# Tokens on 128 partitions with the last 64 apart, and batch 1's queries in 512-byte pieces turned by TensorE, in a fused packed-attention and expert kernel on one core

## The chip, the core and the metric

The kernel runs on one core of a Trainium2 chip. The metric is the device time of one execution in microseconds (us). Before the change it is 443.84 us, the median of three runs (443.28 to 444.25). Engines are named as in the profile: PE is TensorE, PEld its weight load, DVE is VectorE, ACT is ScalarE, POOL is GpSimd, SP is SyncE (here it issues nearly every DMA).

## What is computed

There are 8 batches, 8 heads, 576 tokens, head width 64. All is float32.

```python
def _attn_ref(q, k, v, p):                 # q, k, v: (8, 8, 576, 64); p: (8, 8, 32, 64)
    p_packed = sm_attn(p, k, v)            # 32 pack queries look at 576 keys
    out = sm_attn(q, p_packed, p_packed)   # 576 queries look at the 32 packed rows
def _moe_ref(x, w_gate, w_local, w1, w2):  # x: (8, 576, 512), the heads side by side
    logits = x @ w_gate                    # 8 experts
    # a token takes its own best expert, or its predecessor's, by a local gate; the first its own
    h = np.maximum(x[b, s] @ w1[e], 0.0)   # w1: (8, 512, 1024)
    out[b, s] = p[e] * (h @ w2[e])         # w2: (8, 1024, 512)
```

## The kernel before

The expert of a batch's first token is read back by the program (`choose`, L641: the number `e` is written by DVE and loaded into a register of SP), and only then can SP ask for that expert's weights. All 576 tokens of the batch are run through this one expert; a branch after the main program redoes what strays from it.

For each batch the work has two sides. The *main* side is the expert: `layer1` (L917) and `layer2` (L945 to L954) over 16 steps, eight chunks of 128 hidden rows for each of two token halves (320 and 256 tokens); `relu` (L928 on ACT, L932 on DVE) stands between them, and `splits` (L903 on ACT, L905 on DVE) makes a high and a low part of each chunk of `w2`. The *side work* prepares a later batch: load (`loads`), turn the keys so that the head width lies on partitions (`turn_keys`, L395 on DVE; for batch 1 `turn_tokens`, L376 on PE and L381 on ACT), `scores` (L428 matmul, L436 and L447 on DVE), `keys` (exponential L464, transposes L474, copies L479, the product with the values L493, normalising L505, transpose L513, copy L514 to `ppT`), turn the queries (`turn_queries`, L527 on DVE; for batch 0 `turn_tokens`), `queries` (L543, L563), the softmax over 32 packed rows (`soften`, L581 to L607, nearly all on DVE), `gates` (L699 to L783, which holds the choice `e`), and `pack_weights` (L877, L888, L891), which multiplies the packed values into `w1`. Batch 0 has its own path: keys turned by DVE (L362), an early choice from token 0 alone (`early_choice`, L654 to L687), `w1` in four quarters (`pack_quarters`, L848 to L860), queries in two parts.

The order of the instructions is not written out. A planner (`Clock`, `weave`) walks generators; each `need(...)` says which tiles, buffers (`slot`) and PSUM banks a step waits for, and the planner gives out the step whose modelled time has come: loads first, then side work, oldest batch first, then the main side. Its prices are a few constants: DMA bytes over `clock.rate` (GB/s), a line for each engine. Each engine then runs what it was given in that order. `BUFS` has the buffers of each tag: `kv` holds keys, values and first queries, `qn` the turned or to-be-turned keys and queries. While the main side has not begun, matmuls on a constant (L216, `keep_warm`) fill PE's gaps.

SP's order of batch 0's weights is the list `FIRST`: `1` a quarter of `w1`, `2` a chunk of `w2`, `v` batch 1's values, `q` half of batch 1's queries. `load_tokens` brings keys or values as 96 partitions of six tokens (1,536-byte pieces), `load_pairs` batch 0's queries as 96 partitions with two tokens side by side (512-byte pieces), `load_blocks` all later queries and keys in 128-byte pieces, already in the blocks that DVE's transpose wants. Three conditions matter here: `turn_keys` waits for `sts[0]["quads"][0] == NQ` (long true after batch 0), `turn_queries` for the tiles `a2t` of its batch, which come free when the batch before has issued its gate matmuls (L699, `give(*a2t)`), and `scores` takes two PSUM banks for each of two head groups `Q`, both at once for batch 1 (four banks).

## Time and profile before

| | us |
|---|---|
| median of 3 runs | 443.84 |
| the profiled execution | 441.43 |
| its span, first to last instruction | 439.7 |
| PE busy (matmuls on the constant among it) | 417.1 (21.5) |
| DVE, ACT, POOL busy | 303.5, 177.1, 27.1 |
| mean granted TensorE clock | 0.984 of full |

A view by windows gives, for each stretch, the busy time of each engine with its number of instructions, then the granted TensorE clock (1.00 is 2.4 GHz, 0.50 is 1.2 GHz), the share of the 16 DMA engines that was busy, and the rate. A line of the timeline has the start, the length, engine, line, operation, tiles, how many were merged, and in brackets how long the engine had sat idle and what ended that. DMA issues appear under the queue that issues them (SPq).

### The profile page before, as it was taken

How to read it: one execution, taken by the hardware profiler on the slowest of the kernel's cores; microseconds unless marked ns; L12 is line 12 of the kernel's file. 1: busy time of each engine (PE TensorE's matmuls, PEld its weight loads, DVE VectorE, ACT ScalarE, POOL GpSimd, SP SyncE). 2: the span in 40 equal slices, each digit the busy share in tenths (PEclk: the TensorE clock that was granted, in tenths of full speed). 3: DMA queues.
4: the chain of work that ended last, by engine and by line, in shares of the span. 5: the costliest groups of instructions: out<-in, count | busy, mean ns of one | idle time of the engine just before them, and what ended most of it. 6: DMA issues, size and time to landing. Idle time of an engine off the chain costs nothing.

```text
span 439.7 us, 10378 instructions
## 1 busy us (share of the span) xinstructions
PE 417.1 (95%) x4030; PEld 335.3 (76%) x4031; DVE 303.5 (69%) x862; ACT 177.1 (40%) x409; POOL 27.1 (6%) x44
## 2 busy tenths in 40 slices
PE   9998999768999989999999899998999999999995
PEld 8886788455887768877887578786887788878884
DVE  4586779848886488777967597747887688537231
ACT  1554533236434352435543353235342553335121
POOL 0000010300020000200020003000011001100000
PEclk9999999958999999999999999999999999999999
DMA  8989999472999479982899669991999640454011
GB/s 187 224 263 234 160 176 133 89 288 97 204 125 249 156 225 151 165 288 82 197 131 163 259 179 167 135 346 61 223 132 159 258 142 6 162 185 145 0 60 54
DMA packets 165078, 73.17 MB, mean 166 GB/s; under 512 B 133024, under 2 KB 145056, under 8 KB 165024
## 3 DMA queue, kind: packets, MB, share of 16 engines
q1 hardware_dynamic: 162752, 72.04, 77.1%
q8 instruction: 33, 0.54, 0.6%
q10 hardware_dynamic: 2272, 0.41, 0.6%
q14 instruction: 21, 0.17, 0.2%
HBM read 63.00 MB, written 9.44 MB: 165 GB/s over the span
## 4 chain that ended last, share of the span: by engine, by line
PE 77%; DVE 9%; DMA 9%; issue 2%; ACT 1%; SPq 1%; POOLq 0%; DVEq 0%; POOL 0%; ACTq 0%
PE bank L945 35%; PE bank L917 20%; DMA w1t<-in_moe_w_dram 4%; PE bank L950 3%; PE bank L954 3%; DMA qn<-in_q_dram 3%; PE bank L216 3%; PE bank L474 2%; PE bank L493 2%; PE bank L543 2%; DVE qn L527 2%; PE bank L428 2%; DVE wpl L891 2%; DMA kv<-in_q_dram 2%; PE bank L877 1%
## 5 line engine op out<-in xcount | busy, mean ns | idle before, releaser
L945 PE MATMUL bank<-w2s,h 128*128 128x512 f32 x768 | 204.0, 398 | 4.2 <-DVE w2s L905 2.5
L945 PEld LDWEIGHTS bank<-w2s,h 128*128 128x128 f32 x768 | 136.1, 188 | 32.7 <-issue 4.0
L932 DVE SCALAR_TENSOR_TENSOR h<-bank,h 128x256 fp32r<-128x256 f32 x192 | 61.5, 348 | 67.5 <-ACT h L928 67.4
L928 ACT ACTIVATE h<-bank 128x256 fp32r<-128x256 f32 (+1 forms) x128 | 52.9, 413 | 133.8 <-PE bank L917 127.5
L917 PEld LDWEIGHTS bank<-a2h,wph 128*128 128x128 f32 x256 | 47.0, 188 | 16.8 <-issue 1.9
L917 PE MATMUL bank<-a2h,wpl 128*128 128x320 f32 (+1 forms) x256 | 56.6, 299 | 2.3 <-DVE wpl L891 2.3
L917 PE MATMUL bank<-a2h,wph 128*128 128x320 f32 (+1 forms) x256 | 56.7, 302 | 0.0
L917 PE MATMUL bank<-a2l,wph 128*128 128x320 f32 (+1 forms) x256 | 54.8, 295 | 0.0
L917 PEld LDWEIGHTS bank<-a2h,wpl 128*128 128x128 f32 x256 | 41.4, 188 | 4.2 <-DVE wpl L891 4.1
L607 POOL TENSOR_TENSOR a2l<-a2t,a2h 128x576 fp32r<-128x576 f32 (+2 forms) x17 | 23.1, 1360 | 330.5 <-ACT a2h L604 255.2
L905 DVE TENSOR_TENSOR w2s<-w2raw,w2s 128x512 fp32r<-128x512 f32 x64 | 41.8, 683 | 0.5 <-ACT w2s L903 0.5
L917 PEld LDWEIGHTS bank<-a2l,wph 128*128 128x128 f32 x256 | 41.0, 188 | 0.0
L903 ACT CAST w2s<-w2raw 128x512 fp32r<-128x512 f32 x64 | 37.6, 623 | 2.6 <-DMA w2raw<-in_moe_w_dram 2.5
L950 PE MATMUL bank<-w2s,h 128*128 128x512 f32 x64 | 25.6, 401 | 0.0
L954 PE MATMUL bank<-w2s,h 128*64 128x512 f32 x64 | 25.0, 390 | 0.0
L216 PE MATMUL bank<-warm 128*128 128x128 f32 x136 | 21.5, 305 | 1.1 <-DVE warm L211 1.1
L216 PEld LDWEIGHTS bank<-warm 128*128 128x128 f32 x136 | 18.9, 214 | 2.4 <-issue 1.6
L464 ACT ACTIVATE a<-a,nb 128x576 f32<-128x576 f32 x16 | 12.4, 777 | 20.5 <-DVE nb L447 20.5
L888 ACT CAST wph<-bank 128x512 fp32r<-128x512 f32 x28 | 15.1, 597 | 11.7 <-PE bank L877 11.5
L563 DVE STREAM_TRANSPOSE sT<-bank 128x288 f32<-128x288 f32 (+2 forms) x36 | 13.0, 417 | 9.0 <-ACT gate L561 9.0
L527 DVE STREAM_TRANSPOSE qn<-qn 128x1152 f32<-128x1152 f32 x14 | 19.1, 1369 | 0.0
L479 ACT COPY a1T<-bank 96x384 f32<-96x384 f32 x30 | 13.1, 477 | 14.4 <-PE bank L474 14.4
(126 smaller groups left out, 431.9 us busy)
## 6 DMA issues: line engine op xcount, KB each, us to landing
w2raw<-in_moe_w_dram SPq DMA_DIRECT2D x64, 256.0 KB, 6.0
w1t<-in_moe_w_dram SPq DMA_DIRECT2D x14, 1024.0 KB, 6.6
kv<-in_v_dram SPq DMA_DIRECT2D x16, 576.0 KB, 8.1
qn<-in_q_dram SPq DMA_DIRECT2D x28, 288.0 KB, 7.1
out_dram<-o SPq DMA_DIRECT2D x31, 256.0 KB, 2.4
qn<-in_k_dram SPq DMA_DIRECT2D x24, 288.0 KB, 8.1
kv<-in_k_dram SPq DMA_DIRECT2D x4, 576.0 KB, 5.7
w1t<-in_moe_w_dram SPq DMA_DIRECT2D x4, 512.0 KB, 7.4
```

The costliest lines, as they stand in the source:

```text
L216: nc.tensor.matmul(out=warm_ps[:, :128], lhsT=warm, rhs=warm, start=True, stop=True)
L527: nc.vector.transpose(out=qT, in_=qT)
L607: eng.tensor_tensor(out=a2l, in0=a2t, in1=a2h.bitcast(F32), op=ALU.subtract)
L888: nc.scalar.copy(out=hi[fh][:, Q], in_=ts[fh, Q])
L903: nc.scalar.copy(out=w[:, 0], in_=raw)
L905: nc.vector.tensor_tensor(out=w[:, 1], in0=raw, in1=w[:, 0].bitcast(F32), op=ALU.subtract)
L917: nc.tensor.matmul(out=t[:, :GROUP * (m1 - m0)], lhsT=st["wp"][c // 4][wi][:, Q, fs], rhs=a2[ai][Q][:, GROUP * m0:GROUP * m1], start=(n == ...
L928: nc.scalar.activation(out=h[:, :w], in_=t[:, :w], func=AF.Relu)
L932: nc.vector.scalar_tensor_tensor(out=h[:, dst:dst + z - a], in0=t[:, a:z], scalar=0.0, in1=h[:, a:z].bitcast(F32), op0=ALU.max, op1=ALU.su ...
L945: nc.tensor.matmul(out=acc, lhsT=hs[hi], rhs=w[:, wi], start=(c == 0 and n == 0), stop=(c == NC - 1 and n == 2),)
L950: nc.tensor.matmul(out=acc, lhsT=h[:, 256:WIDE + TAIL], rhs=w[:, 0], start=(c == 0), stop=False, skip_group_check=True,)
L954: nc.tensor.matmul(out=acc[0:TAIL], lhsT=h[:, 256:WIDE], rhs=w[:, 1], start=False, stop=(c == NC - 1), skip_group_check=True,)
```

## The change

Keys, values and batch 0's queries are loaded as 128 partitions of four tokens for the first 512 tokens (1,024-byte pieces; queries and batch 1's keys in two DMAs of 512-byte pieces), and the last 64 tokens apart (`rest`): one DMA more for each load, into tiles under the tag `o`, or for values into constant tiles `v_rest` whose upper half GpSimd clears once at the start. The score row is cut into four chunks of 128 and one of 64 instead of six of 96: five transposes for a head group instead of six, the copies redrawn (for batches from 1 on one of 128x512 and one of 64x128 instead of two of 96x384), and five chunks instead of six in the product with the values. Batch 0's scores go over four row groups instead of three, with extra matmuls for the last 64 tokens.

Batch 1's queries are no longer brought in 128-byte pieces inside `FIRST`; they are loaded after its keys by `load_pairs` and turned by PE and ACT (`turn_tokens`), and need not wait for `a2t`. `FIRST` has the values earlier, before the third and fourth quarter of `w1`. `kv` has five buffers. Batch 1's scores are given out for each head group by itself (two banks). From batch 2 on the turning of keys and queries waits until the choice of the batch before has been given out. Batch 0's `w2` chunks from the third on have their low part made by GpSimd. A copy of 8 logits in `early_choice` is gone. Batch 0's packs come in four copies, and three small loads move from ACT's queue to SP's, behind the values.

```diff
@@ BUFS, FIRST
-    "kv": 4, "qn": 3, ...
+    "kv": 5, "qn": 3, ...
-FIRST = "1 2 1 2 2 1 2 v 1 2 q 2 q 2 2".split()
+FIRST = "1 2 1 2 2 v 1 2 1 2 2 2 2".split()
...
@@ load_tokens (load_pairs alike, in two DMAs of 512-byte pieces and a rest)
-        x = tile_([TP, HQ, NJ * D], F32, "kv")
-        clock.rate = 255.0
-        nc.sync.dma_start(
-            out=x, in_=at(src, b).rearrange("(h q) (p c) d -> q p h (c d)", q=NQ, c=NJ)[Q],
-        )
-        return x
+        x = tile_([128, HQ, NJ * D], F32, "kv")
+        rest = tile_([TAIL, HQ, D], F32, "kt", "o") if rest is None else rest
+        rows = at(src, b).rearrange("(h q) s d -> q h s d", q=NQ)[Q]
+        clock.rate = 340.0
+        nc.sync.dma_start(out=x, in_=rows[:, 0:512].rearrange("h (p c) d -> p h (c d)", c=NJ))
+        clock.rate = 200.0
+        nc.sync.dma_start(out=rest[0:TAIL], in_=rows[:, 512:S].rearrange("h p d -> p h d"))
+        return x, rest
...
@@ loads
-            order = (("p", 1), ("k", 0), ("k", 1)) if st["second"] else \
+            order = (("p", 1), ("k", 0), ("k", 1), ("q", 0), ("q", 1)) if st["second"] else \
                 (("v", 0), ("v", 1), ("p", 1), ("k", 1), ("q", 1))
...
@@ turn_tokens
-        yield need(slot="qn", when=lambda: (name, 0) in st and (name == "k" or "a2t" in st))
+        yield need(slot="qn", when=lambda: (name, 0) in st and (st["second"] or "a2t" in st))
...
-                for c in range(J3):
+                for c in range(2):
...
+                nc.tensor.transpose(out=tp[:, 256:HALF], in_=rest[:, h], identity=ident[:TAIL // 2, :TAIL // 2])
...
@@ turn_keys, turn_queries
-            yield need(when=lambda: "k" in st and "p" in st and (not isinstance(st["b"], int) or sts[0]["quads"][0] == NQ))
+            yield need(when=lambda: "k" in st and "p" in st and (not isinstance(st["b"], int) or "ereg" in sts[st["b"] - 1]))
...
-        yield need(when=lambda: "q" in st and "a2t" in st)
+        yield need(when=lambda: "q" in st and "a2t" in st and (not isinstance(st["b"], int) or "ereg" in sts[st["b"] - 1]))
...
@@ keys
-            for c in range(NJ):
+            for c in range(NJ + 1):
...
-                        lhsT=a1T[Q][:, c, 32 * h:32 * h + 32],
-                        rhs=st["v", Q][:, h, D * c:D * c + D],
-                        start=(c == 0), stop=(c == NJ - 1),
+                        lhsT=(a1T[Q][:, c] if c < NJ else a_rest[Q])[:, 32 * h:32 * h + 32],
+                        rhs=st["v", Q][0][:, h, D * c:D * c + D] if c < NJ else st["v", Q][1][:, h],
+                        start=(c == 0), stop=(c == NJ),
...
@@ splits
-            nc.vector.tensor_tensor(out=w[:, 1], in0=raw, in1=w[:, 0].bitcast(F32), op=ALU.subtract)
+            (nc.gpsimd if st["early"] and c > 1 else nc.vector).tensor_tensor(out=w[:, 1], in0=raw, in1=w[:, 0].bitcast(F32), op=ALU.subtract)
...
@@ weave
-                    *(scores(st, Qs) for Qs in apart), *(keys(st, Qs) for Qs in apart),
+                    *(scores(st, Qs) for Qs in (apart if started != 1 else ((0,), (1,)))), *(keys(st, Qs) for Qs in apart),
...
-                    *((turn_tokens(st, "q"),) if early else (turn_queries(st, Q) for Q in both)),
+                    *((turn_tokens(st, "q"),) if started < 2 else (turn_queries(st, Q) for Q in both)),
```

## Rows read from the trace of the kernel before

**Rows 1.** The page's first part: busy time, share of the span and instructions of each engine.

```profile
PE 417.1 (95%) x4030; PEld 335.3 (76%) x4031; DVE 303.5 (69%) x862; ACT 177.1 (40%) x409; POOL 27.1 (6%) x44
```

**Rows 2.** The view by windows of 5 us, in the start, in batch 0's main work and between batch 0 and batch 1: stretch and its length, PE, PEld, DVE, ACT, POOL busy, granted clock, DMA share, GB/s.

```profile
20.00:25.00 5.00, 4.73 (x70) 3.73 (x70) 4.33 (x20) 3.16 (x10) 0.00 (x0) 1.00 0.86 227
...
35.00:40.00 5.00, 4.23 (x40) 3.25 (x39) 4.85 (x13) 3.10 (x8) 0.00 (x0) 1.00 1.09 240
...
70.00:75.00 5.00, 5.00 (x30) 4.36 (x29) 4.61 (x9) 2.37 (x5) 0.00 (x0) 1.00 1.06 126
...
80.00:85.00 5.00, 3.94 (x61) 2.66 (x59) 3.36 (x10) 0.95 (x2) 1.42 (x2) 1.00 0.29 89
85.00:90.00 5.00, 1.71 (x21) 1.13 (x22) 4.89 (x18) 1.28 (x5) 0.37 (x2) 0.78 0.13 29
90.00:95.00 5.00, 3.67 (x73) 2.85 (x75) 2.49 (x18) 2.59 (x6) 0.00 (x0) 0.50 1.05 397
```

**Rows 3.** The timeline of PE at the end of batch 0's main work and at the start of batch 1's.

```profile
80.75 1.56 PE L945 MATMUL bank<-w2s,h 128*128 128x512 f32 x6
...
99.92 2.70 PE L877 MATMUL bank<-w1t,ppT 64*32 64x512 f32 x32
...
102.55 0.76 PE L917 MATMUL bank<-a2h,wph 128*128 128x320 f32 x2
...
105.40 1.55 PE L945 MATMUL bank<-w2s,h 128*128 128x512 f32 x6
```

**Rows 4.** The timeline of DVE before batch 1's choice (L641), the SP queue's first issue of that expert's weights (L827), and the page's group for the low parts of `w2` (busy, mean ns of one, idle before), and its line for the loads of `w1` (count, size of each, us from issue to landing).

```profile
58.89 1.38 DVE L527 STREAM_TRANSPOSE qn<-qn 128x1152 f32<-128x1152 f32 x1
...
78.64 1.37 DVE L395 STREAM_TRANSPOSE qn<-qn 128x1152 f32<-128x1152 f32 x1
...
83.36 0.40 DVE L362 STREAM_TRANSPOSE p_in<-p_in 128x256 f32<-128x256 f32 x1
...
84.00 1.37 DVE L395 STREAM_TRANSPOSE qn<-qn 128x1152 f32<-128x1152 f32 x1
...
85.37 1.37 DVE L527 STREAM_TRANSPOSE qn<-qn 128x1152 f32<-128x1152 f32 x1
...
86.85 0.14 DVE L641 TENSOR_SCALAR e<-codes_all 1x1 int32<-1x1 f32 x1
...
87.80 1.02 SPq L827 DMA_DIRECT2D w1t<-in_moe_w_dram  x2
...
L905 DVE TENSOR_TENSOR w2s<-w2raw,w2s 128x512 fp32r<-128x512 f32 x64 | 41.8, 683 | 0.5 <-ACT w2s L903 0.5
...
w1t<-in_moe_w_dram SPq DMA_DIRECT2D x14, 1024.0 KB, 6.6
```

**Rows 5.** The timeline of batch 0's gate matmuls, which set the `a2t` tiles free, and of batch 1's softmax, first operation.

```profile
55.44 0.65 PE L699 MATMUL bank<-a2t,gate 128*32 128x128 f32 x16
...
67.37 1.57 DVE L563 STREAM_TRANSPOSE sT<-bank 128x288 f32<-128x288 f32 x4
```

**Rows 6.** PE's timeline of the side work of a batch where the clock is full: scores, transposes of one head group, the product with the values, the queries (of batch 1), and the packing of `w1`.

```profile
134.99 1.20 PE L428 MATMUL bank<-qn,p_in 64*32 64x288 f32 x32
...
138.33 0.82 PE L474 MATMUL bank<-ident,a 128*96 128x128 f32 x6
...
143.24 1.55 PE L493 MATMUL bank<-kv,a1T 96*32 96x64 f32 x96
...
65.55 1.20 PE L543 MATMUL bank<-qn,ppT 64*32 64x288 f32 x32
...
146.32 1.95 PE L877 MATMUL bank<-w1t,ppT 64*32 64x512 f32 x32
```

**Rows 7.** The timeline of the start: batch 0's first scores, the turning of one head by PE, the issue of the last quarter of `w1`, the first matmul of layer 1, matmuls on the constant after it, and the packing of the last quarter.

```profile
9.34 1.15 PE L428 MATMUL bank<-kv,p_in 32*32 32x192 f32 x48
...
26.94 0.41 PE L376 MATMUL bank<-ident,kv 96*128 96x96 f32 x3
...
31.00 0.72 SPq L809 DMA_DIRECT2D w1t<-in_moe_w_dram  x1
...
32.29 0.56 PE L917 MATMUL bank<-a2h,wph 128*128 128x320 f32 x2
...
36.70 1.60 PE L216 MATMUL bank<-warm 128*128 128x128 f32 x12
...
43.59 0.67 PE L848 MATMUL bank<-w1t,ppT 64*32 64x256 f32 x16 [0.71 <-DMA w1t<-in_moe_w_dram]
```

**Rows 8.** The view by windows of 1 us, columns as in rows 2: keys and values on 96 partitions, batch 0's queries on 96 partitions in 512-byte pieces, a pause of the DMA engines, a stretch with a quarter of `w1` on 128 partitions, and batch 1's values on 96 partitions.

```profile
10.00:11.00 1.00, 1.00 (x29) 0.69 (x18) 1.00 (x2) 0.00 (x0) 0.00 (x0) 1.00 1.11 224
...
16.00:17.00 1.00, 1.00 (x75) 1.00 (x75) 0.62 (x4) 0.00 (x0) 0.00 (x0) 1.00 1.20 254
...
24.00:25.00 1.00, 1.00 (x12) 1.00 (x12) 1.00 (x4) 0.80 (x2) 0.00 (x0) 1.00 0.35 84
...
27.00:28.00 1.00, 1.00 (x12) 1.00 (x11) 1.00 (x5) 0.80 (x3) 0.00 (x0) 1.00 1.08 374
...
35.00:36.00 1.00, 0.33 (x3) 0.14 (x1) 1.00 (x5) 0.90 (x3) 0.00 (x0) 1.00 1.10 245
```

**Rows 9.** The timeline of POOL: two subtractions of a low part, one in batch 0's main work and one later.

```profile
78.24 1.78 POOL L607 TENSOR_TENSOR a2l<-a2t,a2h 128x576 fp32r<-128x576 f32 x1 [21.79 <-ACT a2h L604]
...
119.89 1.43 POOL L607 TENSOR_TENSOR a2l<-a2t,a2h 128x576 fp32r<-128x576 f32 x1 [31.70 <-ACT a2h L604]
```

More of the change, by code (lines that the diff above doesn't have):

```diff
@@ L328, in loads @@
         if st["early"]:
[L329 to L335 removed]
+            st["p"] = load_packs(b, (nc.sync, nc.scalar, nc.sync, nc.scalar))
             order = (("k", 0), ("k", 1), ("v", 0), ("v", 1), ("q", 0), ("q", 1))
@@ L352, in loads @@
                 st[name] = load_blocks(x, b)
-            else:
-                st[name, Q] = load_pairs(x, b, Q) if name == "q" else load_tokens(x, b, Q)
+            elif name == "v":
+                st[name, Q] = load_values(b, Q)
+            else:
+                st[name, Q] = load_tokens(x, b, Q) if name == "k" and st["early"] else load_pairs(x, b, Q)
+            if st["early"] and (name, Q) == ("v", 1):
+                clock.rate = 100.0
+                with nc.allow_non_contiguous_dma(reason="512 elements"):
+                    nc.sync.dma_start(out=q0[:, :, 0:1], in_=q[0, :, 0:1, :].rearrange("h s d -> d h s"))
+                    nc.sync.dma_start(out=wgl[:, :, 0:E], in_=w_gate.rearrange("(h d) e -> d h e", d=D))
+                    nc.sync.dma_start(out=wgl[:, :, E:E + 1], in_=w_local.rearrange("(h d) e -> d h e", d=D))
         if st["second"]:
-            yield need(when=lambda: "q" in st and len(sts[0]["w2"]) == NC)
+            yield need(when=lambda: ("v", 1) in st and len(sts[0].get("w2", ())) == NC)
         st["loaded"] = True
@@ L398, in turn_keys @@
             yield need(when=lambda: ("k", Q) in st and "p" in st)
-            yield need(st["k", Q])
-            turn(st["k", Q])
-            st["kT", Q] = st["k", Q].rearrange("a h (c x i) -> a h x c i", c=NJ, x=2)
+            yield need(*st["k", Q])
+            for x in st["k", Q]:
+                turn(x)
+            st["kT", Q] = st["k", Q][0].rearrange("a h (c x i) -> a h x c i", c=NJ, x=2)
         if Q == 0:
@@ L433, in scores @@
                         )
+            for x in range(steps if st["early"] else 0):
+                for r in range(2):
+                    ps_ = slice(rows * r, rows * r + rows)
+                    for h in range(HQ):
+                        nc.tensor.matmul(
+                            out=ts[Q, r][32 * h:32 * h + 32, 128:160],
+                            lhsT=st["pT"][ps_, NQ * h + Q, x],
+                            rhs=st["k", Q][1][ps_, h, NP * x:NP * x + NP],
+                            start=(x == 0), stop=(x == steps - 1),
+                        )
         for Q in Qs:
             for r in range(n):
+                w = HALF if n == 2 else 160 if r < 2 else 128
+                out, t = parts(sc[Q], r), ts[Q, r][:, :w]
                 nc.vector.tensor_scalar(
-                    out=parts(sc[Q])[r], in0=ts[Q, r][:, :S // n].rearrange("a (c i) -> a c i", i=NP),
-                    scalar1=-SCALE, scalar2=None, op0=ALU.mult, op1=ALU.min, accum_out=m3[Q][:, r:r + 1],
+                    out=out, in0=t if n == 2 else t.rearrange("a (c i) -> a c i", i=NP),
+                    scalar1=-SCALE, scalar2=None, op0=ALU.mult, op1=ALU.min, accum_out=m4[Q][:, r:r + 1],
                 )
```

124 lines of the change are left out of this document (59 added, 65 removed), and 2 rows, old and new, of the table BUFS.

## The prediction

> **What bounds the kernel now.** I read the page's busy shares first: PE is busy for 95% of the span [rows 1], so it looks full. But 21.5 us of that is the constant's matmuls, so the windows come next. From 110 us on PE is dense; what is lost lies in three places. (a) The start: the first matmul of layer 1 comes at 32.29 us [rows 7]. (b) Batch 0's first half, where PE has gaps and still runs the constant, as in the window from 35 us [rows 2, 7]. (c) The gap between batch 0 and batch 1, in the windows from 80 us on [rows 2]: PE is busy for 1.71 us of 5, and the granted clock falls from 1.00 to 0.50 (from 2.4 to 1.2 GHz) after PE fell idle.
>
> The last group of batch 0's layer 2 begins at 80.75 and ends at about 82.3; batch 1's layer 2 begins at 105.40 [rows 3]. These 23.1 us hold work too. At the full clock it is: batch 1's gate matmuls 0.96 (the 0.65 of such a group [rows 5] and 0.31 for its short second half); batch 2's scores 1.20, transposes 2 x 0.82, product 1.55, a transpose 0.4, queries 1.20 and 0.3 of gate weights; packing 1.95 [rows 6]; two chunks of layer 1, 2 x 0.88. Sum 11.0, so **12.1 us are lost there**.
>
> Why does PE wait there? Follow the choice back. The choice is written at 86.85, SP asks for the weights at 87.80, packing starts at 99.92 [rows 3, 4]. The chain before it is batch 1's softmax on DVE, from 67.37 on [rows 5], and in DVE's order work stands in the chain that has nothing to do with it: batch 2's keys and packs turned at 78.64, 83.36 and 84.00, batch 2's queries at 85.37; earlier batch 1's own queries, in two such turns from 58.89 on, and the low parts of `w2` at 0.683 each [rows 4].
>
> **The change part by part.**
>
> *(A) Start.* Batch 0's loads run with the DMA engines saturated: 224 GB/s for keys and values on 96 partitions, 254 for the queries, 245 for batch 1's values, at a share over 1; a quarter of `w1` on 128 partitions moves at 374 with the same share [rows 8]. I take 340 for the 128-partition parts. Then 2.06 MB of keys and values take 6.1 us where 9.2 were needed, but 0.26 MB of rests comes at an unknown rate: between 112 (half of 224, for half the partitions) and 254; I take 200, 1.3 us. The new row group count makes batch 0's scores 48 matmuls for each head group instead of 24; 24 show as 48 records in 1.15 us [rows 7], nearly all of it by count and not by columns, so each gets 0.5 to 0.9 us longer on the path. Against that: key turns shorter by 0.2 each (1,024 and 256 columns for 1,536), one wait of PE for the queries (0.5) gone, one transpose less, 0.2 for the logits' copy. DVE is busy for 4.33 of the 5 us from 20 on [rows 2], so early queries save no more than its holes, 0.7 in 5, about 2 up to 32 us. I take layer 1's start 1.3 us earlier, 31.0; bounds 2.8 earlier (all holes closed) and 1.5 later (loads as slow as before; 1.15 MB of batch 1's queries now stand ahead of the first quarter of `w1`, and the pause of the DMA engines around 24.5 us [rows 8] takes up only a part).
>
> *(B) Gaps in batch 0.* In 34.8 to 44.2 PE loses 0.77, then 1.4 in the constant, then 0.71 waiting for the last quarter of `w1` [rows 2, 7], 2.9 in all. That quarter was issued at 31.00 and landed near 43.5, behind 4.25 MB. With values at 340 instead of 245 it lands some 1.5 to 4 us earlier, and 128-byte pieces no longer follow it. Gain 1.5, bounds 0 and 2.8. Behind the late quarter, DVE and ACT stand in order, with batch 0's second softmax after it; that helps (C).
>
> *(C) The choice.* From DVE's path before 86.85 go: two turns of batch 1's queries 2.74; three turns of batch 2 and its packs 4.51, which now wait for the choice; six low parts 4.10 [rows 4]. Sum 11.35. If DVE bounds all of it and (A) and (B) come along, the choice moves to 86.85 - 11.35 - 2.8 = 72.7; if only the four operations in line from 78.64 on count, to 82.3. DVE is busy for 4.61 of the 5 us from 70 on [rows 2], which is nearer to a bound than to a line of waits, so I take that end, 73. The softmax can also start earlier: batch 1's scores need two free banks instead of four, its values come sooner, its queries are turned off DVE, so what is left is `a2t`, free at 55.44, while the softmax started at 67.37 [rows 5]; that is cover for the estimate. The packing follows the choice by 13.1 us in this trace, but there PE first ran batch 2's work at half clock; such a load lands 6.6 us after its issue [rows 4], the second issue 0.5 to 1 later, so packing can start at 73 + 0.95 + 1 + 6.6 = 81.5. Batch 0's main work ends at 82.3 - 1.3 - 1.5 + 1.3 (D less E's first batch) = 80.8. The casts behind packing take 2.6 [rows 3]; part of it lies behind batch 1's gates and leftover chunks. I leave **2.0 lost of 12.1: gain 10.1**, bounds 12.1 (nothing lost) and 2 (choice at 82.3: packing at 91).
>
> *(D) Batch 1's queries on PE.* 24 transposes, 0.41 for three [rows 7], so 3.3 us, and 8 copies of 0.4 on ACT, which is half idle. If they fall into the time before layer 1 they replace the constant and cost nothing. I take 1.8 lost, bounds 0 and 3.3.
>
> *(E) Fewer chunks.* For each batch from 1 on: ten transposes instead of twelve, 2 x 0.137 = 0.27; 40 matmuls instead of 48 with the values, 1.55 x 8/48 = 0.26 [rows 6]. PE is the bound there, so 0.53 x 7 = **3.7**; bounds 2 (the chunks are read with a stride, and PE's order shifts) and 4.5. ACT's copies (512 and 128 columns for two of 384) and the two score ops, which now write every second element, I cost at nothing: both engines have room there.
>
> *(F) Low parts on GpSimd.* POOL takes 1.43 to 1.78 for 576 columns [rows 9], so 1.3 to 1.6 for 512, against 0.683; six of them, one for each chunk of 2.7 us on PE. Nothing, as long as the chunk is there early; if each delays its chunk, 6 x 0.8 = 4.8.
>
> *(G) Later batches.* Holding back the turning of batch b's keys to the choice of b - 1 costs nothing: batch 3's scores, at 134.99 [rows 6], already stood behind batch 2's choice, as the scores of every later batch do in this trace. SP gets two more issues for each load of values, some 0.8 us a batch, behind which the pieces of keys and queries wait; bounds 0 and 0.5 a batch, taken as 0.
>
> Sum: -1.3 - 1.5 - 10.1 + 1.8 - 3.7 = -14.8 on the profiled 441.43 (439.7 span and 1.73 around it): 426.6. The median of the runs lies 2.4 above the profiled execution, so **429.0**.
>
> **A rule against it.** What the rows show: 128 partitions at 374 GB/s, 96 at 224 to 254, at equal DMA share [rows 8]. The Trainium skill, "DMA: Bandwidth & Descriptors", section "Why a DMA increments its semaphore by 16 and not by 1", has a 96-partition tile spread over 16 engines just as a 128-partition one. By that rule alone 128 partitions bring no rate, and (A) and (B) lose their ground; the traces differ also in which load it is, so the rule is not refuted here. As a mechanism of this kernel it is rival 2.
>
> **The rivals.**
> 1. *The choice stays late* (82 rather than 73). For it: batch 1's softmax starts behind batch 0's gates, and everything before them depends on batch 0's second softmax, which this change touches least. Against: 7.25 of the 11.35 stand directly among the last 30 us. Then 10 us stay lost, 429.0 + 8 = **437**.
> 2. *Loads stay at 240.* 6.3 MB instead of 5.05 stand ahead of `w1`: 1.2 MB at 230 is 5.4 us, of which the DMA pauses near 19 and 25 us take up about 3. Layer 1 starts at 33.5 instead of 31.0, the last quarter gains nothing (+1.5): **433**.
> 3. *The values block SP (slower).* In `FIRST` the values now stand before the third and fourth quarters of `w1`. Their second half needs the `kv` buffer of batch 1's first keys, so SP waits until PE and ACT have turned those, and behind it wait both quarters and five chunks of `w2`. The planner puts batch 1's work last before layer 1. The last quarter leaves SP at 31.00 now, right behind the values [rows 7]; with some 5 us of room, each us past 36 costs one, since all of batch 0 and the choice shift. The point from which it decides is 36 + 14.8 = 50.8. If the turning is given out only with batch 0's gates (55.44 [rows 5]), it is 429.0 + 19.4 = **448**. Against: in the trace such turns run at 26.94 [rows 7], before layer 1, and they wait for no other engine than PE and ACT.
>
> **How the numbers follow.** Forecast 0.62, rival 1 0.18, rival 2 0.11, rival 3 0.09. The forecast's own bounds, not all bad at once, are 421 to 434; rival 1 carries the upper end to 440. Range 421 to 440, leaving out rival 3 and the ends. 0.2% (0.9 us) is about what a measurement of this kernel can tell from no change. Faster takes the first three cases but for a sliver of rival 1: 0.88. Same 0.03, slower 0.09.
>
> **What would show it.** Layer 1 starts near 31; the last quarter of `w1` lands before 41; no turn of queries or keys of batch 2 stands on DVE ahead of batch 1's choice, which is written near 73 and before 76; PE keeps the full clock between the batches; ten transposes and 80 records of the product for each batch. Wrong it is if the choice comes after 80, if SP issues the third quarter after 36, or if PE waits for `w2` low parts on POOL.

## The result, and the profile after

The changed kernel takes **431.29 us** (median of 4 runs, 431.04 to 431.77), the kernel before, run beside it, 443.56 (441.38 to 444.25): ratio 0.9733, 95% interval 0.9698 to 0.9768. Forecast were 429.0 and a range of 421 to 440. The profiled execution took 431.04; its span is 429.0, 10.7 less than before.

Four marks tell most of where that comes from: the start of layer 1 of batch 0; the first operation of batch 1's softmax on DVE; batch 1's choice; the start of batch 1's layer 2. The first lines are PE's timeline of the kernel after, in the start and between the batches.

```profile
14.72 0.32 PE L453 MATMUL bank<-kt,p_in 32*32 32x32 f32 x22 [2.11 <-issue]
...
24.97 0.24 PE L392 MATMUL bank<-ident,qt 32*128 32x32 f32 x1 [0.29 <-DMA qt<-in_k_dram]
...
33.30 0.66 PE L870 MATMUL bank<-w1t,ppT 64*32 64x256 f32 x16
...
38.18 0.56 PE L939 MATMUL bank<-a2h,wph 128*128 128x320 f32 x2
...
87.38 1.66 PE L967 MATMUL bank<-w2s,h 128*128 128x512 f32 x6
89.00 0.74 PE L497 MATMUL bank<-ident,a 128*128 128x128 f32 x4
89.58 0.27 PE L501 MATMUL bank<-ident,a 128*64 128x128 f32 x1
89.78 1.95 PE L899 MATMUL bank<-w1t,ppT 64*32 64x512 f32 x32
91.81 0.89 PE L939 MATMUL bank<-a2h,wph 128*128 128x320 f32 x2
...
93.72 1.54 PE L967 MATMUL bank<-w2s,h 128*128 128x512 f32 x6
```

Its first line shows a hole: PE stands idle for 2.11 us in the middle of batch 0's second scores, and the releaser is "issue", nothing that the profile names. Layer 1 starts at 38.18, **5.9 later** than before [rows 7], and batch 1's layer 2 at 93.72, 11.7 earlier [rows 3]. Between the two batches PE now goes from one piece of work to the next: batch 0's layer 2 ends at 89.04, and packing follows at 89.78. The windows of the kernel after (columns as in [rows 2]) say the same; the clock stays at 1.00:

```profile
20.00:25.00 5.00, 4.63 (x90) 3.18 (x90) 1.99 (x9) 2.25 (x8) 0.00 (x0) 1.00 0.75 209
35.00:40.00 5.00, 5.00 (x70) 3.04 (x69) 3.70 (x11) 3.19 (x9) 0.00 (x0) 1.00 1.10 323
70.00:75.00 5.00, 5.00 (x30) 4.26 (x29) 4.45 (x13) 2.27 (x6) 0.00 (x0) 1.00 0.83 177
80.00:85.00 5.00, 4.81 (x27) 3.85 (x27) 3.96 (x18) 1.13 (x5) 0.37 (x2) 1.00 0.41 98
85.00:90.00 5.00, 5.00 (x60) 3.33 (x66) 4.72 (x18) 1.47 (x4) 0.00 (x0) 1.00 1.05 398
90.00:95.00 5.00, 4.66 (x44) 2.45 (x29) 4.37 (x10) 4.58 (x11) 0.00 (x0) 1.00 0.38 136
```

DVE's timeline of the kernel after answers to [rows 4, 5]: the softmax begins 4.7 us earlier, the choice comes 6.0 earlier, and batch 2's turns stand behind the choice.

```profile
27.37 0.14 DVE L669 TENSOR_SCALAR e<-ecd 1x1 int32<-1x1 f32 x1
...
62.64 1.58 DVE L591 STREAM_TRANSPOSE sT<-bank 128x288 f32<-128x288 f32 x4 [0.74 <-ACT gate L589]
...
80.85 0.14 DVE L669 TENSOR_SCALAR e<-codes_all 1x1 int32<-1x1 f32 x1
82.67 1.37 DVE L408 STREAM_TRANSPOSE qn<-qn 128x1152 f32<-128x1152 f32 x1
```

The marks of all kernels whose times tell something, from their profiled executions (us); "main" is from the start of batch 0's layer 1 to that of batch 1's layer 2, "rest" from there to the end of the span. Ratios are to the kernel before in the same series; its medians in the five series are 440.27 to 443.56, the last beside the kernel after. Against the others 431.29 would be 0.976 to 0.980, so ratios of different series compare only roughly.

| kernel | ratio (95%) | median | profiled | layer 1 | softmax | choice | main | rest |
|---|---|---|---|---|---|---|---|---|
| before | 1 | 443.56 | 441.43 | 32.29 | 67.37 | 86.85 | 73.1 | 334.3 |
| after | 0.9733 (0.9698-0.9768) | 431.29 | 431.04 | 38.18 | 62.64 | 80.85 | 55.5 | 335.2 |
| e4 conditions alone | 0.9943 (0.9898-0.9989) | 439.45 | 440.26 | 31.87 | 68.46 | 84.97 | 69.5 | 337.1 |
| e11 and queries on PE | 0.9820 (0.9763-0.9876) | 434.29 | 435.37 | 34.69 | 62.35 | 82.93 | 61.7 | 337.2 |
| e5 low parts on DVE | 0.9858 (0.9814-0.9902) | 436.15 | 436.95 | 39.66 | 65.18 | 84.80 | 59.9 | 335.5 |
| e1 small loads on ACT | 0.9799 (0.9714-0.9884) | 432.89 | 432.86 | 39.67 | 64.13 | 82.33 | 55.5 | 335.6 |
| e2 wide constant | 0.9929 (0.9886-0.9972) | 437.76 | 436.99 | 37.15 | 67.22 | 84.83 | 62.4 | 335.3 |
| e7 both exponentials first | 0.9774 (0.9690-0.9859) | 432.64 | 433.10 | 38.76 | 62.57 | 81.47 | 57.5 | 334.8 |
| e3 queries turned late | 0.9854 (0.9810-0.9897) | 435.74 | 438.41 | 41.08 | 69.00 | 87.42 | 59.8 | 335.4 |
| e6 old order of loads | 0.9812 (0.9767-0.9857) | 433.78 | 438.46 | 43.81 | 69.52 | 87.80 | 57.2 | 335.3 |
| e12 keys on 96 | 0.9911 (0.9871-0.9951) | 437.01 | 437.03 | 44.05 | 68.52 | 86.72 | 55.5 | 335.4 |
| e14 e12, choice first | 0.9844 (0.9805-0.9883) | 434.73 | 438.06 | 42.41 | 68.48 | 86.66 | 57.1 | 336.5 |
| e15 choice first | 0.9983 (0.9955-1.0011) | 439.96 | 439.95 | 37.90 | 69.99 | 87.58 | 64.3 | 335.6 |

Medians and ratios leave out the executions in a slower state that this program sometimes shows; the marks are from one execution each, and those of e3, e6 and e14 took 2.7, 4.7 and 3.3 us longer than their median, so that their marks can show losses which the median does not hold.

The span is the sum of layer 1, main and rest: in the kernel after, these differ by +5.9, -17.6 and +1.0. The shortest main, 55.5, is shared by three kernels. No kernel has a lower median than the one after; the intervals of e1, e6, e7 and e11 overlap with its own.

### The profile page after: what moved, and what is told of

It reads as the page before. It is cut to its first block, busy times and chain, and to the rows that moved or that the text cites. A ratio compares the mean times of both kernels' runs of the same rounds, so it can differ in the third digit from the quotient of the medians.

```text
span 429.0 us, 10275 instructions
## 1 busy us (share of the span) xinstructions
PE 413.5 (96%) x3958; PEld 329.0 (77%) x3959; DVE 295.4 (69%) x859; ACT 178.8 (42%) x419; POOL 36.3 (8%) x56
## 4 chain that ended last, share of the span: by engine, by line
PE 73%; DMA 9%; DVE 8%; SPq 6%; issue 2%; ACT 1%; POOLq 0%; DVEq 0%; POOL 0%; ACTq 0%
PE bank L967 33%; PE bank L939 19%; DMA qn<-in_q_dram 6%; SPq L307 4%; PE bank L972 3%; PE bank L976 3%; DVE wpl L913 2%; PE bank L571 2%; PE bank L521 2%; PE bank L899 2%; PE bank L443 2%; DVE qn L555 1%; PE bank L497 1%; DMA kv<-in_q_dram 1%; PE bank L391 1%
## 5 line engine op out<-in xcount | busy, mean ns | idle before, releaser
L967 PE MATMUL bank<-w2s,h 128*128 128x512 f32 x768 | 207.3, 400 | 3.9 <-DVE w2s L927 3.2
L927 DVE TENSOR_TENSOR w2s<-w2raw,w2s 128x512 fp32r<-128x512 f32 x58 | 37.4, 680 | 1.3 <-ACT w2s L925 1.3
L972 PE MATMUL bank<-w2s,h 128*128 128x512 f32 x64 | 25.3, 396 | 0.0
L913 DVE TENSOR_TENSOR wpl<-bank,wph 128x512 fp32r<-128x512 f32 x28 | 18.0, 680 | 2.4 <-ACT wph L910 2.4
L910 ACT CAST wph<-bank 128x512 fp32r<-128x512 f32 x28 | 14.9, 595 | 10.8 <-PE bank L899 10.8
L463 DVE TENSOR_SCALAR_CACHE_REDUCE a<-bank 128x288 f32<-128x288 f32 (+2 forms) x36 | 13.6, 421 | 6.0 <-PE bank L453 3.8
L632 ACT CAST a2h<-a2t 128x576 fp32r<-128x576 f32 (+2 forms) x18 | 11.2, 622 | 13.8 <-DVE a2t L626 9.5
L214 PE MATMUL bank<-warm 128*128 128x128 f32 x88 | 15.8, 335 | 1.1 <-DVE warm L209 1.1
```

The costliest lines, as they stand in the source:

```text
L214: nc.tensor.matmul(out=warm_ps[:, :128], lhsT=warm, rhs=warm, start=True, stop=True)
L913: nc.vector.tensor_tensor(out=lo[fh][:, Q], in0=ts[fh, Q], in1=hi[fh][:, Q].bitcast(F32), op=ALU.subtract)
L927: (nc.gpsimd if st["early"] and c > 1 else nc.vector).tensor_tensor(out=w[:, 1], in0=raw, in1=w[:, 0].bitcast(F32), op=ALU.subtract)
L967: nc.tensor.matmul(out=acc, lhsT=hs[hi], rhs=w[:, wi], start=(c == 0 and n == 0), stop=(c == NC - 1 and n == 2),)
L972: nc.tensor.matmul(out=acc, lhsT=h[:, 256:WIDE + TAIL], rhs=w[:, 0], start=(c == 0), stop=False, skip_group_check=True,)
```

## The experiments

**Where the gain comes from.** e4 is the kernel before with the two conditions of the change alone:

```diff
-            yield need(when=lambda: "k" in st and "p" in st and (not isinstance(st["b"], int) or sts[0]["quads"][0] == NQ))
+            yield need(when=lambda: "k" in st and "p" in st and (not isinstance(st["b"], int) or "ereg" in sts[st["b"] - 1]))
...
-        yield need(when=lambda: "q" in st and "a2t" in st)
+        yield need(when=lambda: "q" in st and "a2t" in st and (not isinstance(st["b"], int) or "ereg" in sts[st["b"] - 1]))
```

> The kernel before with one part of the change alone: the turning of keys and queries of a batch waits for the choice of the batch before. Theory 1 (the gap between batch 0 and 1 was made by batch 2's four operations standing on DVE in front of batch 1's choice): the choice comes 4.5 us earlier or more, at 82.4 or before, gates and packing move into batch 0's main work, at most 3 of the 12.1 us in the gap stay lost, and the time falls by 8 to 11 us, to 433 to 436. Rival (the choice comes early only with batch 1's queries loaded early and turned off DVE): the choice moves by 3 us or less, the gap keeps 9 or more of its 12.1, the time falls by 0 to 3 us.

Choice at 84.97, 1.9 earlier than before, ratio 0.9943, or 2.5 us: the rival's figures hold. Batch 2's packs are turned after the choice now, and PE waits for just that; the clock is at 0.50 behind this wait. PE's timeline and windows of e4:

```profile
88.58 1.41 PE L428 MATMUL bank<-qn,p_in 64*32 64x288 f32 x16 [4.28 <-DVE p_in L362]
```

```profile
85.00:90.00 5.00, 1.41 (x16) 0.43 (x16) 4.08 (x13) 0.34 (x2) 0.37 (x2) 0.73 0.53 182
90.00:95.00 5.00, 1.41 (x17) 0.42 (x18) 4.88 (x19) 0.87 (x2) 0.00 (x0) 0.50 1.04 392
```

e11 adds batch 1's queries on TensorE (and its scores in two halves), still on 96 partitions:

```diff
-FIRST = "1 2 1 2 2 1 2 v 1 2 q 2 q 2 2".split()
+FIRST = "1 2 1 2 2 1 2 v 1 2 2 2 2".split()
...
-            order = (("p", 1), ("k", 0), ("k", 1)) if st["second"] else \
+            order = (("p", 1), ("k", 0), ("k", 1), ("q", 0), ("q", 1)) if st["second"] else \
...
-                    *((turn_tokens(st, "q"),) if early else (turn_queries(st, Q) for Q in both)),
+                    *((turn_tokens(st, "q"),) if started < 2 else (turn_queries(st, Q) for Q in both)),
```

> The kernel before with two parts of the change: nothing of batch 2's keys and queries is turned until batch 1's choice, and batch 1's queries come in 512-byte pieces and are turned by TensorE (scores of batch 1 in two halves). Keys, values and first queries stay on 96 partitions, the low parts on DVE. Theory (the gain comes from what leaves DVE ahead of the choice: 2.74 us of query turns on top of what the conditions alone brought, choice at 84.97): choice at 79 to 82, layer 1 of batch 0 at 32.5 to 34, the gap between the batches 3 to 6 us of lost PE time instead of 12.1, total 432 to 436. Rival (the 128 partitions carry the gain, by earlier loads and fewer chunks): choice 83 to 85, total 438 to 441.

Ratio 0.9820: about 0.7 of the gain without 128 partitions. The total lies in the theory's range, choice and layer 1 just outside. The choice comes only 2.0 earlier than in e4, but the softmax 6.1 earlier, and the wait between the batches is gone. What main still has over 55.5, 6.2 us, lies earlier: PE idles for 2.22 us before the last quarter of `w1` and for 1.67 us with no releaser, and the clock falls behind both (0.66 in the window from 45, 0.81 and 0.85 in those from 60 and 65). PE's and SP's timelines of e11:

```profile
46.04 1.11 PE L848 MATMUL bank<-w1t,ppT 64*32 64x256 f32 x16 [2.22 <-DMA w1t<-in_moe_w_dram]
61.86 0.26 PE L553 MATMUL bank<-wgl,ppT 64*32 64x9 f32 x10 [1.67 <-issue]
```

```profile
19.82 5.28 SPq L283 DMA_DIRECT2D kv<-in_q_dram  x6
26.16 0.44 SPq L809 DMA_DIRECT2D w1t<-in_moe_w_dram  x1
```

SP's lines show a cost: the early choice is written at 22.84, but SP issues batch 1's queries until 25.1, so `w1` is asked for 3.3 us after the choice (1.17 in the kernel before).

e5 is the kernel after with the low parts on DVE again (`nc.vector` in place of the choice of engine in `splits`).

> The changed kernel, but the six low parts of w2 go back from GpSimd to DVE (0.68 us each there). Theory (DVE bounds batch 1's choice): choice 2 to 4 us after the 80.85 of the changed kernel, a gap of that size less 0.3 opens between batch 0 and batch 1, total 433 to 435. Rival (by now DVE has room between 40 and 58 us, where it is busy for about 7 of 10): choice within 1 us, total 431 to 432.

Choice at 84.80, 3.95 later: the theory holds for the choice, though 1.5 of that comes with a later layer 1, and the total of 436.15 lies 1.2 above its range. The clean pair is e5 and e1, whose layer 1 starts at the same time (39.66 and 39.67): with the low parts on DVE the choice is 2.5 later and main 4.4 longer. The gap opens again, as PE's timeline of e5 shows: batch 2's transposes stand ahead of the packing in PE's order and wait for an exponential whose keys were turned after the late choice.

```profile
94.08 1.13 PE L497 MATMUL bank<-ident,a 128*128 128x128 f32 x4 [2.99 <-ACT a L488]
```

Before, e4, e11, e5 and after stand in a row, so main can be priced in steps: the conditions take 3.6 us off it, batch 1's queries on PE 7.8, the step from e11 to e5 (128 partitions, the order of the loads and the rest of the change) 1.8, and the low parts on GpSimd 4.4. The third step gains nothing that shows: layer 1 starts 5.0 later in e5 than in e11, the rest is 1.7 shorter, and the median is 436.15 for 434.29 (executions 435.38 to 436.95 and 433.06 to 436.32). So no run shows that the 128 partitions shorten the whole. e11 with the low parts on GpSimd, which might be faster than the kernel after, was not run.

**Why layer 1 starts late.** Four kernels change the kernel after: e1 issues the three small loads on ACT's queue; in e2 the constant's matmuls are 256 wide and half as many; in e7 batch 0's transposes wait for both exponentials again; e6 loads batch 1's values behind the last quarter of `w1`. The edits of e1 (one line of three), e2, e7 and e6:

```diff
+                nc.scalar.dma_start(out=q0[:, :, 0:1], in_=q[0, :, 0:1, :].rearrange("h s d -> d h s"))
...
-WARM, FILL = 10, 240.0
+WARM, FILL = 5, 480.0
...
-            yield need(sc, banks=2)
+            yield need(sc, banks=2, when=lambda: not st["early"] or st["weighed"] == NQ)
...
-FIRST = "1 2 1 2 2 v 1 2 1 2 2 2 2".split()
+FIRST = "1 2 1 2 2 1 2 v 1 2 2 2 2".split()
```

> The changed kernel with the three small loads (one query, two gate weights) back on ACT's queue at the start. Theory 1 (PE runs out of instructions in the second scores, at a fixed place of its program, 111 matmuls in): PE's idle time of 2.2 us inside the second scores stays at the same instruction, at 1.5 us or more, and layer 1 starts within 1 us of 38.2; time within 1 us. Rival (the small loads hold up SP's queue and the DMA engines, and with them PE): the idle time goes, layer 1 starts 2 to 3.5 us earlier, and the time falls by 2 to 3.5 us.

> The changed kernel with half as many matmuls on the constant, each twice as wide (256 columns): the same busy time of PE, some 50 instructions fewer ahead of the second scores. Theory 1 (PE runs out of instructions): the idle time leaves the second scores and stands after them, 111 matmuls into the program as before; the second scores end 1.5 to 2.2 us earlier, layer 1 starts 1 to 2 us earlier, the time falls by 1 to 2 us. Rival (PE is held up by the DMA traffic of the small loads at 12.6 to 14.7 us): the idle time stays at that time of the span and nothing moves by more than 0.5 us.

> The changed kernel with the old condition back that batch 0's transposes wait for both exponentials. Theory 1 (ACT does the first head group's two copies before the second exponential, and so the second group's packed values come late): the second exponential starts about 1 us earlier, layer 1 about 1 us earlier, time down by 0.5 to 1.5 us. Rival (the second group waits for its scores on PE anyway, and the first group gains from going ahead): no change within 0.5 us, or up to 1 us slower.

> The changed kernel, but batch 1's values are asked for after the last quarter of w1, as before, not ahead of the third. Theory (the last quarter is no bound any more, since layer 1 itself starts at 38): third and fourth quarter are issued 4 to 5 us earlier, layer 1 stays at 38 within 0.5, no PE time is won in 38 to 50, total 430.5 to 432. Rival (the late quarters delay the packing, and with it batch 0's first half and second softmax): batch 1's choice 1.5 to 3 us earlier than 80.85, total 428.5 to 430.

Only e2 starts layer 1 earlier than the kernel after, by 1.0, and no total of the four falls in the range of its theory: e1 keeps the hole, 432.89; e7 starts the second exponential 0.5 earlier, at 16.86, and gains nothing, 432.64; e2 loses 6.9 in main, with the choice 4.0 later, 437.76. In e6's profiled execution the clock was at 0.50 in the windows from 30 to 40 and layer 1 came at 43.81, so its marks don't tell what the order of the quarters does; its median of 433.78 misses both ranges.

These marks can't be compared with those of the kernel after without a look at the clock. There it is granted at 1.00 behind the hole; in e1, e2, e5 and e7 it falls to 0.50 for a while, and in e15 too (0.72 in the same window). Windows of the kernel after, then of e1:

```profile
15.00:20.00 5.00, 4.13 (x77) 3.57 (x69) 2.81 (x16) 2.26 (x8) 0.00 (x0) 1.00 0.93 227
```

```profile
15.00:20.00 5.00, 4.44 (x81) 4.21 (x81) 1.80 (x12) 0.89 (x3) 0.00 (x0) 0.66 0.95 190
```

e5 shows how much that can be worth. Its edit lies behind the start, yet its hole is 3.49 us long, its clock falls too (0.66), and layer 1 comes 1.5 later, as in e1. So e1 and e7 (hole and low clock too) are no clean tests of their edits.

All four have PE's hole. It is 3.15 us in e1, 3.13 in e7, 2.51 in e6, and in all three behind the **111th matmul** of the program, counted in program order. With half the constants that is no longer a score but a transpose, and the hole goes there. In this the theories of e1 and e2 held. PE's timeline of e2:

```profile
15.50 1.09 PE L497 MATMUL bank<-ident,a 128*128 128x128 f32 x4 [2.55 <-issue]
```

All eight kernels with batch 0's keys on 128 partitions have it, 2.1 to 3.5 us; none of the five others in the table, which get there after 16 us. The trace names no releaser. But the times of a DMA queue called "instruction" fit: its first packet of 16 KB within the span has landed at 12.99 to 14.02 us in the eight, and PE goes on 1.25 to 1.88 us after that in each. In the five others it has landed 1.55 us or more before PE gets to that place. The hole of 1.67 us in e11, at another place of the program, ends 1.69 us after such a packet. That TensorE runs out of instructions fits all of this; no run changed their supply, and the trace doesn't say for which engine a packet is, so it is argued, not shown.

e13 tried it from the other side: the kernel before with the constant's matmuls 32 columns wide and planned four times as many.

> The kernel before, but the constant's matmuls have 32 columns instead of 128 and are planned four times as many, so 119 matmuls instead of 50 are issued up to the end of the first scores; loads, keys on 96 partitions and all else as before. Theory (a stop at a fixed place of the program, about the 111th matmul, whatever the work there): PE stands idle for 1 to 4 us with no releaser inside or right around the first group of 24 score matmuls, which this kernel runs from 9.34 us on without a hole; layer 1 later than 32.29 by 1 to 4. Rival (the stop belongs to the keys' rests or to 128 partitions): no such idle time, scores as before.

It tells nothing of the hole: its one execution took 530.4 us. The constant alone ran to 41.8 us, since 190 records of 32 columns took 40.74 us, 0.21 each, more than the 0.13 of 128 columns [rows 7]. The scores came long after the time of the hole in the others.

e12 takes the hole away: keys of batch 0 on 96 partitions, 24 score matmuls for a head group, results written in the order of the tokens.

```diff
+        x = tile_([96, HQ, 6 * D], F32, "ke", "qn")
...
+        nc.sync.dma_start(out=x, in_=at(k, b).rearrange("(h q) (p c) d -> q p h (c d)", q=NQ, c=6)[Q])
...
-        n = 4 if st["early"] else 2
+        n = 3 if st["early"] else 2
...
+                return x[:, 0:S].rearrange("a (r i c) -> a r c i", r=3, c=6)[:, r]
```

> The changed kernel, but batch 0's keys come on 96 partitions again, without rests (24 score matmuls for each head group instead of 48; their results are written in the order of the tokens, so values, queries and chunks stay as changed). The 111th matmul of the program then lies in the first product, not in the second scores. Theory (TensorE stops for 2.1 to 3.5 us at its 111th matmul when it gets there before about 14 us, and this stop with the doubled score matmuls makes most of the 5.9 us by which layer 1 starts late): no idle time of PE without a releaser before 16 us, batch 0's early choice 2 to 4 us earlier than 27.37, layer 1 at 34 to 36.5, total 426.5 to 430. Rival (the start is late because of the loads: small ones on SP, the keys' rests and 1.15 MB of batch 1's queries ahead of w1): layer 1 at 37.5 or later, total 431 to 434, keys at 224 GB/s coming on top.

The hole is gone, the early choice comes at 27.43 all the same, and layer 1 at 44.05; the total of 437.01 lies above both ranges. PE's timeline and windows of e12:

```profile
23.18 0.33 PE L398 MATMUL bank<-ident,kv 128*128 128x128 f32 x1 [1.00 <-DMA kv<-in_k_dram]
23.97 0.47 PE L398 MATMUL bank<-ident,kv 128*128 128x128 f32 x1 [0.46 <-DMA kv<-in_k_dram]
```

```profile
20.00:25.00 5.00, 3.55 (x41) 2.20 (x39) 1.72 (x8) 2.02 (x7) 0.00 (x0) 0.85 0.89 232
25.00:30.00 5.00, 5.00 (x38) 2.57 (x37) 2.23 (x9) 1.90 (x5) 0.00 (x0) 0.50 1.03 250
```

Ahead of the choice PE waits for batch 1's keys, and in this window with 3.55 us of work the clock falls, to 0.50 (1.2 GHz) up to 40.6 us. So e14 (on e12) and e15 (on the kernel after) let batch 1's turns begin only when the early choice has been read:

```diff
-        yield need(slot="qn", when=lambda: (name, 0) in st and (st["second"] or "a2t" in st))
+        yield need(slot="qn", when=lambda: (name, 0) in st and ((st["second"] and "ereg" in sts[0]) or "a2t" in st))
```

> As the run with batch 0's keys on 96 partitions, and besides batch 1's keys and queries are turned on TensorE only once batch 0's early choice has been read, so that no wait of PE for batch 1's loads (1.00 and 0.46 us at 23 to 24 us in that run) stands ahead of it. Theory (that run had lost the stop of PE at its 111th matmul, but gave it back because PE then waited for batch 1's keys and the clock was granted at 0.50 from 24 to 40 us): clock 1.00 up to 50 us, early choice 24 to 25.5 instead of 27.43, layer 1 at 35 to 37 instead of 44.05, total 427 to 430.5. Rival (the loads set the start): choice at 27 or later or layer 1 at 38 or later even at the full clock, total 431 or more.

> The changed kernel with that last edit alone: batch 1's keys and queries are turned on TensorE only once batch 0's early choice has been read (batch 0's keys on 128 partitions with the stop of PE at its 111th matmul). Theory (batch 1's turns and their wait for the rest of the keys at 24.97 stand ahead of the early choice and cost about 1 us of the 5.9): early choice 26 to 26.8 instead of 27.37, layer 1 37 to 37.8 instead of 38.18, total 429.5 to 431. Rival (the turns only fill time in which PE waits anyway): choice and layer 1 within 0.3, total 431 to 433, more if the order of batch 1's turns now delays its scores.

In e14 the choice moves to 25.48, and layer 1 doesn't follow. SP's and PE's timelines of e14:

```profile
26.02 2.32 SPq L298 DMA_DIRECT2D qt<-in_q_dram  x1
29.41 0.40 SPq L832 DMA_DIRECT2D w1t<-in_moe_w_dram  x1
```

```profile
33.67 1.11 PE L866 MATMUL bank<-w1t,ppT 64*32 64x256 f32 x16 [2.42 <-DMA w1t<-in_moe_w_dram]
```

SP is still issuing batch 1's queries, so the first quarter of `w1` is asked for 3.9 us after the choice; PE idles for it, and the clock falls (0.51 in the window from 35). The clock isn't all of it: an execution of e14 with a mean clock of 0.999 still took 432.81, and the median, 434.73, is in the rival's range. In e15 choice and layer 1 are within 0.3 of the kernel after, as the rival has it; but since its clock fell behind the hole and that of the kernel after didn't, a gain of the size of the theory (about 1 us) can be hidden there: with the clock low as well, e1 and e5 have their early choice at 28.86 and 28.85, e15 at 27.60. What it costs is plain: batch 1's turns go into batch 0's main work, batch 1's softmax starts 7.4 later, and nearly the whole gain is gone. e3, which moves only the queries' turns, also delays the softmax:

```diff
-        yield need(slot="qn", when=lambda: (name, 0) in st and (st["second"] or "a2t" in st))
+        yield need(slot="qn", when=lambda: (name, 0) in st and ((st["second"] and (name == "k" or "begun" in sts[0])) or "a2t" in st))
```

> The changed kernel, but batch 1's queries may be turned on TensorE only after batch 0's layer 1 has begun. Theory (batch 1's turns on PE stand ahead of layer 1 and cost part of the 5.9 us by which it starts later): layer 1 starts 1.5 to 2.5 us earlier than the 38.18 of the changed kernel, near 36; five of the eight groups (0.55 us each) then come among batch 0's main work, so batch 0's end moves by at most 0.8 and the total is 430.5 to 432. Rival (the turns only fill time in which PE would run the constant): layer 1 stays within 0.5 of 38.2, the constant takes the place of the turns, and the total grows by the 2.7 us of the moved groups, 433 to 434.

Layer 1 at 41.08 instead of 36: with fewer turns ahead of it, PE had 4.35 and 4.07 us of work in the two windows from 20 on, and the clock was at 0.57 from 30 to 35. The queries turned late then hold up the softmax (69.00), and 435.74 lies above both ranges. An execution of e3 with a mean clock of 0.997 still took 434.82, so the clock is not what makes it slower than the kernel after.

## Why the prediction was right, and which steps were wrong

The total was met within 2.3 us, in part by luck: errors offset each other. Against the forecast, layer 1 came 7.2 later, main was 7.3 shorter, and the rest 4.2 longer (2.9 of it moved there from main, see (C)). So the profiled execution took 431.04 where the sum said 426.6, 4.4 more; the 2.4 added for the median, which in the kernel after lies only 0.25 above the profiled execution, made half of that good.

**(A) failed, in sign.** Forecast was layer 1 1.3 earlier; it is 5.9 later, outside the bounds. The step looked at bytes and rates, and left out what PE and ACT do in between. The early choice is 4.1 later than before (27.37 for 23.27), and 3.9 of that stands already at the second exponential; from the choice to layer 1 it takes 10.8 instead of 9.0. ACT's timeline before, then after:

```profile
13.47 0.78 ACT L464 ACTIVATE a<-a,nb 128x576 f32<-128x576 f32 x1 [0.60 <-DVE nb L447]
```

```profile
16.38 0.37 ACT L503 COPY a1T<-bank 128x256 f32<-128x256 f32 x1 [3.84 <-PE bank L497]
17.33 0.78 ACT L488 ACTIVATE a<-a,nb 128x576 f32<-128x576 f32 x1
```

Three things stand behind this in the traces. The hole, 2.11 us: the step doubled the count of score matmuls and priced them at 0.5 to 0.9 us, not at a stop; in e12, without the hole, the second exponential starts at 15.52. ACT's order: the first group's copies now stand ahead of that exponential (e7 turned this round and gained nothing, with a hole 1.0 longer). And batch 1's turns in PE's order: the packing of the first quarter starts 0.98 us after its landing, 0.36 before. How the 5.9 divides among these stays open.

SP's issues of batch 1's queries are not among them. The prediction had them as a clause ("1.15 MB of batch 1's queries now stand ahead of the first quarter of `w1`") with a bound of 1.5; SP is done with them at 26.9, before the choice, and asks for `w1` 1.17 us after the choice, as before (SP's timeline before, then after; the quarter lands 3.7 and 3.8 us later):

```profile
24.44 0.44 SPq L809 DMA_DIRECT2D w1t<-in_moe_w_dram  x1
```

```profile
28.54 0.40 SPq L836 DMA_DIRECT2D w1t<-in_moe_w_dram  x1
```

They bind as soon as the choice comes earlier: removing one limit lets the next one bind. Without the hole (e12) PE waits for keys; without that wait (e14) SP is late with `w1`. Asking for the first quarter of `w1` ahead of batch 1's queries wasn't tried.

The loads themselves got faster, but less than taken (340): between 4 and 11 us the windows of the kernel after have 258 to 359 GB/s, 308 in the mean; those of the kernel before, on 96 partitions and with small loads among them, 138 to 322, 235 in the mean. The 224 of [rows 8] is one of these. Batch 0's last values landed 1.6 us earlier (12.99 for 14.56), but its second half of the keys only with its rest at 9.09, where it had landed at 9.05 before, so the scores had nothing of it. The sum in (A) also puts the 0.26 MB of rests on the new side alone, though the kernel before loads these tokens too. The view by windows of 1 us, kernel after:

```profile
6.00:7.00 1.00, 1.00 (x6) 1.00 (x6) 0.56 (x1) 0.00 (x0) 0.00 (x0) 1.00 1.05 359
8.00:9.00 1.00, 1.00 (x11) 1.00 (x9) 1.00 (x3) 0.00 (x0) 0.00 (x0) 1.00 1.04 341
9.00:10.00 1.00, 1.00 (x71) 0.78 (x69) 1.00 (x2) 0.00 (x0) 0.00 (x0) 1.00 1.14 284
```

And in the kernel before, with keys on 96 partitions under way (they landed at 6.48 and 9.05):

```profile
4.00:5.00 1.00, 1.00 (x7) 1.00 (x6) 0.00 (x0) 1.00 (x1) 0.00 (x0) 1.00 1.10 322
5.00:6.00 1.00, 1.00 (x7) 1.00 (x6) 0.00 (x0) 0.20 (x1) 0.00 (x0) 1.00 1.11 281
```

So rival 2 (loads stay at 240) was wrong on its rate, though layer 1 came later than it said. The Trainium skill's rule beside it ("DMA: Bandwidth & Descriptors", both shapes on 16 engines) doesn't settle the rate; another page bears on it. The Trainium skill, "SBUF — State Buffer", section "Door 1: The DMA port swizzle (why `[64,N]` ≈ `[32,N]`)", lists which partitions share a port: by it, 96 partitions put eight on each of eight ports and four on each of the others. An estimate from that page is that 96 are as slow as 128 with three quarters of the bytes, 280 for the 374 GB/s of [rows 8]. The 224 to 254 of [rows 8] lie below it, the 322 and 281 just shown don't, so the runs don't settle what the number of partitions does to the rate.

**(C) held in its direction and was too small; its claim that DVE bounds all of it failed.** From layer 1 to batch 1's layer 2 it takes 17.6 us less. Of that 2.9 is only moved: batch 2's side work leaves the gap, and the rest is 1.0 longer although (E), by the estimate below, saves 1.9 there. So 14.7 are won, where B, C, D and E's first batch had 1.5 + 10.1 - 1.8 + 0.5 = 10.3. The choice came at 80.85, not 73, and by the text's own test ("if the choice comes after 80") that is a miss; but measured from layer 1 it is 11.9 earlier, close to the 11.35 us of DVE work taken off its path. That the two agree is partly luck, for the parts don't. Most is won ahead of the softmax: from layer 1 to its first operation it takes 24.5 instead of 35.1, 10.6 less, where 6.84 us of DVE work went; from there to the choice 18.2 instead of 19.5, 1.3 less, though the four operations in that stretch were worth 4.51 [rows 4]. So in that last stretch DVE did not bound the choice, though the step had assumed that when it took 73. The runs one part at a time, measured from layer 1: the conditions bring the choice 1.5 earlier (4.51 of DVE work), the queries on PE 4.9 (2.74), the low parts on GpSimd 2.5 (4.10), and the step from e11 to e5 3.1. Rival 1 (choice late, 10 us lost) had the choice's time nearly right and its price wrong: batch 0's main work ended 6.7 later too, and only the distance of the two counts. In the whole time the conditions are worth 0.6% (e4) and the queries on PE another 1.2% (e11).

**(B) and (D)** were not measured alone. What (B) was to remove is gone: PE waits for no quarter of `w1` any more and is busy without a break from 35 to 40, while e11 still loses 2.22 us to the last quarter. But its mechanism failed: the last quarter did not land before 41, as forecast, but at 45.97 (43.46 before), and PE came to it later, since layer 1 itself starts 5.9 later. Three of the eight groups of (D) fall behind the start of layer 1.

**(E)** was 3.7 and is smaller. Kernels with four chunks have a rest of 334.8 to 336.5, those with six and the same order of side work 337.1 and 337.2 (e4, e11): **1.9** from e11 to the kernel after, for six batches and part of another, and 0.6 to 2.4 over all pairs. It had taken the count of instructions. From start to next start the product takes 1.26 where it took 1.48 in e11, 0.22 less and not 0.26, and five transposes take 0.51 where six took 0.57: 0.06 for each group, not 0.137.

**(F)** cost nothing, as forecast (1.28 to 1.53 us each on POOL), and **(G)** nothing that shows in the rest. Rival 3 (values block SP) did not come: the third quarter of `w1` left SP at 36.13, just past the 36 from which it was to cost and which the prediction had named as a sign of being wrong, and PE waited for no quarter, because layer 1 itself had moved to 38.

## What to carry to other kernels

Measure a stage from its own start: here layer 1 came 5.9 later and the choice, counted from it, 11.9 earlier; only the difference of two marks showed that the step worked. Before forecasting a faster start, list per queue (SP, ACT, PE) what the change puts ahead of the one operation everything waits for; bytes and rates alone gave the wrong sign. And where PE lives on filler, moving work can cost the clock: the profiled executions of e3, e6, e12 and e14 ran part of the start at 0.50, those of e1, e2, e5, e7 and e15 a stretch behind the hole, so look at the granted clock before taking a later mark for the price of an edit. Price parts of a change that come together one by one, too: the 128 partitions, which gave this change its name, belong to the one step that shows no gain.

## What the runs showed of the hardware

- PE stood still for 2.1 to 3.5 us behind the 111th matmul (222 records of matmuls, as many of weight loads) in eight kernels that got there before 13 us, whether the next one was a score or a transpose. It went on 1.25 to 1.88 us after the landing of a 16 KB packet on the "instruction" queue; so it did (1.69) behind the hole of e11.
- A fp32 matmul of 32 columns on the constant cost 0.21 us a record in e13; one of 128 columns 0.13 at 36.7 us of the kernel before, and about 0.15 and then 0.09 in its first 9 us (6 to 7 records in each us from 2 to 6, 11 from 6 to 9).
- In e12, e3 and e6 the granted clock was 0.50 for 17.1, 6.8 and 13.7 us of the start. PE's longest idle times ahead of that were 1.00, 2.74 and 2.51 us, and in the windows within it PE counts as fully busy: the busy share alone hides it. The length of an idle time alone doesn't tell: behind its hole the clock fell in e2 (2.55 us) and stayed at 1.00 in e3 (2.74).
